# Spectra and tables of pairs requested seven slots ahead, and tables and planes in six common buffers

## The chip, the cores and the metric

The kernel runs on one core of one Trainium2 chip. The core has TensorE (PE in the profile; PEld are its weight loads), VectorE (DVE), ScalarE (ACT), GpSimd (POOL) and SyncE (SP), an SBUF of 128 partitions, PSUM banks of 2 KB a partition, and 16 DMA engines. SP and POOL issue nearly all transfers of this kernel, each on a queue of its own, in the order of their programs. The metric is the device time of one execution in microseconds; less is better.

## The reference

Two layers. The first is a long convolution by FFT with a filter that a small network makes, the second a feed-forward network (FFN) with the maximum of three products:

```python
h_filt = (np.maximum(pos_emb @ w1, 0.0) @ w2) * np.exp(-0.01 * pos)[:, None]
u = x * v                                            # (4, 12544, 128)
Uf = np.fft.rfft(u, n=2 * S, axis=1)
Hf = np.fft.rfft(h_filt, n=2 * S, axis=0)
y = np.fft.irfft(Uf * Hf[None], n=2 * S, axis=1)[:, :S]
a = (x * y).reshape(4 * 12544, 128)
h = np.maximum(np.maximum(a @ W1, a @ W2), a @ W3)   # W: 128 x 768
out = h @ w_out                                      # 768 x 128
```

Everything is float32.

## The kernel before

**The transform.** The FFT is written as matmuls. A batch's tokens are cut into 98 blocks of 128; 32 *units* of four channels each are multiplied, turned and taken through a first transform over the blocks (90 frequencies, kept as the SBUF tile `spec`). Then 45 *pairs* of frequencies (`NK = 45`) go one by one through a second transform, the product with the filter's spectrum, and the inverse of the second transform; its result is stored in DRAM (`zd`). A tile of the FFN later loads what it needs of it (`zt`), does the last inverse step and runs the FFN on 392 columns.

**The stages.** The first batch's transform stands alone, up to about 296 us. Then the main loop runs over the 32 tiles of each of batches 0, 1 and 2, with six FFN chunks a tile: 192 *slots* a batch. Beside the FFN of one batch the transform of the next is woven in, slot by slot. The last batch's FFN follows alone, from about 1780 us.

**The order is written by hand.** `conv_steps` makes a list of steps for each slot: `at(slot, late, fn, ...)` puts a function into a slot; the main loop emits a slot's FFN work first and then the slot's steps (steps with `late` 0 before those with 1). Every engine runs its instructions in that order. In a batch's 192 slots the units come first (the early part of each stage), then the pairs: `start(x)` gives pair x its slot, the same one for an even x and the odd one after it. So the pairs go two by two, about 5.1 slots from one two to the next; the first two are at slot 59 in the stage beside batch 0, at 58 in the others, the last at 175. Where this document counts j, it counts these twos, and calls each "pair j" for short.

**What a pair step needs.** `g_quarter(g, z)` (L537) does the matmuls of the second transform for pair g (L547, reads `sq` and `wt`) and the inverse for pair z = g - 3 (L557, reads `wt` and the folded product). Three transfers feed a pair:

- `w_load(x)` (L506): the table `wt` of 256 KB from DRAM, one DMA on POOL's queue for each pair; both halves are used at slot `start(x)`.
- `q_load(g, n)` (L512): the spectra `sq` of two pairs, copied within SBUF from `spec` with the parts laid on the partitions that the matmuls want; eight DMAs of 64 KB on SP's queue. It has two buffers. For g = 0 the last unit's `u_fours`, two to three slots before, must have written `spec`.
- `h_load(g, n)` (L526): the filter's spectrum `ht` of two pairs, four DMAs of 256 KB on SP's queue, two buffers, asked for one slot ahead. It is first read by VectorE's `q_re` (L591).

On SP's queue the tiles' `zt` loads stand between these (L782, L789), emitted at the first slot of a tile two tiles ahead, and their two buffers come free when `t_last` of two tiles earlier is done. On POOL's queue stand the tables, the stores `zd` (L580) and `out_dram` (L857), and the loads `xT` (L772), among POOL's own additions (L599, which wait for VectorE's L596).

**The buffers.** `wt` has a pool of three buffers. `u_planes` (L407) makes for each unit a tile of 16-bit planes from the products, which a transposing DMA (L420) reads; these have three buffers under the tag `pl`. Both kinds of tile take 2 KB a partition.

Of the kernel before, what the change touches and what calls it, by code (L numbers as in the profile page):

```python
# [10 lines left out]
FP32 = mybir.dt.float32  # L11
I32 = mybir.dt.int32
U16 = mybir.dt.uint16
# [3 lines left out]
P = 128  # L17
# [78 lines left out]
def kernel(  # L96
# [21 lines left out]
    NK = N1 // 2  # L118
# [287 lines left out]

    def u_planes(u):  # L407
        a, _ = us.pop(u)
        pl_ = cvp.tile([P, 2, 4, P], U16, tag="pl", name="planes", bufs=3)
        w = pl_[:].rearrange("p h s (e m) -> p h s e m", e=2)  # L410
        nc.gpsimd.memset(pl_[:].rearrange("p h s (e m) -> p (h s e) m", e=2)[:, :, HB:], 0)
        for h in range(2):
            nc.gpsimd.tensor_copy(  # L413
                w[:, h, :, :, 0:HB],
                a[:].bitcast(U16).rearrange("p s (m e h) -> p h s e m", e=2, h=2)[:, h])
        us[u] = pl_
# [87 lines left out]
            fn()  # L504

    def w_load(x):  # L506
        w = wp.tile([P, 2, 2, 2, 64], FP32, tag="w", name="wt")
        nc.gpsimd.dma_start(w[:].rearrange("p a k r m -> p (a k r m)"),
                            wq_d[x].rearrange("p a f -> p (a f)"))
        ws[x, 0], ws[x - LATE, 1] = w[:, 0], w[:, 1]  # L510
# [153 lines left out]
    def conv_steps(b, done):  # L664


        out = []

        def at(slot, late, fn, *args):
            out.append((slot, late, len(out), fn, args))  # L670

        for u in range(5, done):
            at(2 * (u - 4), 1, u_first, u)
        lead, low, UNIT = (-14, -NT * NF, 0.8) if b > 1 else (6, 0, 0.7)
        share = UNIT * (NU - done - 1)
        per_pair = (END - lead - 11) / (share + (NK + LATE) // 2 * 2 - 2)
        units = []
        for u in range(done, NU):  # L680
            s = (u - done) * UNIT * per_pair + lead
            load_ = max(low, int(s) - 9)
            at(load_, 0, u_load, b, u)
            mul = max(load_ + 2, int(s) - 6)
            at(mul, 0, u_mul, u, nc.gpsimd)
            at(max(mul, int(s) - 5), 0, u_planes, u)
            at(max(mul + 1, int(s) - 4), 0, u_dma, u)
            at(int(s), 0, u_join, u)
            if u % 2:
                on = int(s + 2)  # L690
                at(on, 1, u_two, u - 1)
                at(on + 1, 1, u_fours, u - 1)
                at(on + 2, 1, u_fours, u)
                units.append(on)
        s0 = on + 7

        def start(x):
            return s0 + int(x // 2 * 2 * per_pair)

        load = [0.6] * (NT * NF)  # L700
        for x in range(NK + LATE):
            s = start(x)
            load[s] -= 1.2
            load[s + 1 + x % 2] += 1.4

        def emptiest(among, cost):
            s = min(among, key=lambda i: load[i])
            load[s] += cost
            return s

        plan = []
        busy = {start(x): 2 for x in range(NK + LATE)}
        for x in range(NK + LATE):
            busy.setdefault(start(x) + 1, 1)
        for s in units:
            for k, n in enumerate((1, 3, 9, 2)):
                busy[s - 1 + k] = max(n, busy.get(s - 1 + k, 0))
        for i in range(NT - 1):
            s = i * NF
            last = min((3, 4, 2), key=lambda k: busy.get(s + k, 0))  # L720
            load[s + last] += 0.6
            if s <= s0:
                plan.append((0, 0, last))
                continue
            a = emptiest(range(s, s + 2), 0.7) - s
            plan.append((a, emptiest(range(s + a, s + max(a + 1, last - 1)), 0.7) - s, last))
        plan.append((3, 3, 4))

        for at_, fn, *args in ((11, h_load, 0, 2), (10, h_load, 2, 2),
                               (9, w_load, 0), (9, w_load, 1), (8, w_load, 2)):  # L730
            at(s0 - at_, 0, fn, *args)
        for x in range(NK + LATE):
            s, odd = start(x), x % 2
            g, z = x if x < NK else None, x - LATE if x >= LATE else None
            at(s, 1, g_quarter, g, z)
            at(s + 1 + odd, 0, g_fold, g, z)
            if x > 2:
                at(s - 4, 0, w_load, x)
            if z is not None:
                at(s + 3 + odd, 0, g_store, b, z)  # L740
            if g is None:
                continue
            if g % 2 == 0:
                at(s - 4, 0, q_load, g, min(2, NK - g))
                if g > 2:
                    at(s - 1, 0, h_load, g, min(2, NK - g))
            first = s + 2 + 2 * odd
            at(first, 0, q_swap, g, 0)
            at(first + 1, 0, q_swap, g, 64)
            last = start(x + LATE) - 1  # L750
            a = emptiest(range(first + 1, min(first + 3, last - 1) + 1), 0.7)
            at(a, 0, q_re, g)
            a = emptiest(range(a, min(first + 4, last - 1) + 1), 0.7)
            at(a, 0, q_im, g)
            two = sorted(emptiest(range(a + 1, last + 1), 0.55) for _ in range(2))
            for q in range(2):
                at(two[q], 0, q_unfold, g, q)
        slots = {}
        for s, _, _, fn, args in sorted(out, key=lambda r: r[:3]):
            slots.setdefault(s, []).append((fn, args))  # L760
        return slots, plan, s0
# [288 lines left out]
    for u in range(4, NU, 2):  # L1050
        t = uts.pop(u)
        for v in range(2):
            if u + 4 < NU:
                u_mul(u + 4 + v)
            at = 4 * (u + v)
# [23 lines left out]
    cvp = pro.enter_context(tc.tile_pool(name="cvp0", bufs=3))  # L1079
# [94 lines left out]
    for s in range(NK + 3):  # L1174
# [34 lines left out]
        if s == NK:  # L1209
            unit(0)  # L1210
            pl = sps.tile([P, 512], FP32, tag="pl", name="pl")
# [23 lines left out]
    wp = conv.enter_context(tc.tile_pool(name="wp", bufs=3))  # L1235
    hh = conv.enter_context(tc.tile_pool(name="hh", bufs=2))
    cvp = conv.enter_context(tc.tile_pool(name="cvp", bufs=3))
# [12 lines left out]
    for b in range(1, B):  # L1250
        slots, *rest = conv_steps(b, EARLY if b == 1 else 0)
        plans.append(rest)
        for s, steps in slots.items():
            besides.setdefault((b - 1) * NT * NF + s, []).extend(steps)
# [145 lines left out]
```

## Time and profile before

| | |
|---|---|
| timed runs | 2223.01, 2230.61, 2232.32 us; median 2230.61 |
| profiled execution | 2221.21 us, its span 2219.4 us, mean granted clock 0.997 |
| 0 to 296 us (first batch's transform alone) | PE busy 281.3 us, DMA share 0.84 |
| 296 to 1780 us (FFN of batches 0 to 2, transform beside it) | PE busy 1478.9 of 1484.0 us, DMA share 0.95, 211 GB/s |
| 1780 us to the end (last batch's FFN) | PE busy 433.9 of 439.4 us, DMA share 0.23 |
| groups L547 and L557 (the matmuls of pairs) | 90.6 and 86.6 us of PE, 2160 matmuls each |
| transfers, issue to landing, median | ht 7.1, wt 5.3, sq 5.6, zt 3.8 us |
| SP's queue | 274.5 MB, 56.6% of the 16 DMA engines' span |
| POOL's queue | 130.3 MB, 21.5% |

A share of busy time is the time in which an engine had an instruction running, over the span. Matmuls are pipelined and the profile models their ends, so PE's gaps are best read from starts. DMA issues are not counted as busy time of the issuing engine; the DMA share is the mean over the 16 DMA engines of the time that packets took, and can pass 1 where packets overlap.

### The profile page before, as it was taken

Reading aid. Unit: us, or ns where it says so; the run is one execution under the profiler, and the core shown is the slowest. Engines: PE = TensorE matmul, PEld = TensorE weight load, DVE = VectorE, ACT = ScalarE, POOL = GpSimd, SP = SyncE. Lnnn points to the kernel's source line nnn. Section 1 sums busy time; section 2 is a strip of 40 time slices with the busy share of each in tenths; the row PEclk is TensorE's granted clock in tenths of the full one; section 3 lists DMA queues with packets and bytes.
Section 4 is the critical chain, followed back from the end, with each engine's and each line's share of the span. In section 5 each row is a group of like instructions: output and inputs, shape, how many; then the busy total and the mean of one; then the engine's idle time right before and its main releaser. Section 6 shows DMA issues by size and latency. Waiting matters only on the chain.

```text
span 2219.4 us, 77166 instructions
## 1 busy us (share of the span) xinstructions
PE 2194.1 (99%) x31655; PEld 1297.3 (58%) x31655; DVE 1534.6 (69%) x3293; ACT 1210.9 (55%) x2223; POOL 1179.0 (53%) x1577
## 2 busy tenths in 40 slices
PE   9999999999999999999999999999999999999999
PEld 7988755555555455555555555555555545667776
DVE  5688857677877766667888766677878744554443
ACT  3699845466666555456666555556666622222222
POOL 1166567534455566544444566634454426666665
PEclk9999999999999999999999999999999999999999
DMA  8789999879999898879999999969999722222221
GB/s 196 186 264 311 291 181 196 171 191 233 247 246 241 218 188 175 168 175 245 230 256 231 229 195 178 173 158 252 236 240 238 200 79 58 59 71 69 63 58 24
DMA packets 491332, 411.62 MB, mean 185 GB/s; under 512 B 289406, under 2 KB 407920, under 8 KB 490979
## 3 DMA queue, kind: packets, MB, share of 16 engines
q1 hardware_dynamic: 443689, 274.50, 56.6%
q0 software_dynamic: 45808, 130.25, 21.5%
q8 instruction: 249, 4.08, 0.8%
q10 hardware_dynamic: 1482, 1.93, 0.4%
q14 instruction: 104, 0.85, 0.1%
HBM read 262.85 MB, written 84.67 MB: 157 GB/s over the span
## 4 chain that ended last, share of the span: by engine, by line
PE 84%; DMA 6%; DVE 3%; POOL 3%; issue 2%; SPq 1%; ACT 1%; POOLq 0%; DVEq 0%; ACTq 0%
PE hps L167 42%; PE ops L167 17%; PE ops L903 6%; PE cps L167 3%; PE cps L449 3%; PE ps L176 3%; PE cps L547 3%; PE cps L557 2%; DMA sq<-spec 2%; DMA ht<-hd 2%; DMA zt<-zd 1%; PE ps L167 1%; DMA wt<-wq_const 1%; POOL xt L638 1%; PE last L167 1%
## 5 line engine op out<-in xcount | busy, mean ns | idle before, releaser
L167 PE MATMUL hps<-gt,w_sb 128*64 128x392 f32 (+1 forms) x7672 | 1157.4, 495 | 0.8 <-DVE gt L829 0.7
L839 ACT ACTIVATE hid<-hps 128x392 f32<-128x392 f32 x768 | 382.5, 498 | 762.7 <-PE hps L167 744.9
L167 PEld LDWEIGHTS hps<-gt,w_sb 128*64 128x64 f32 (+1 forms) x7672 | 430.6, 126 | 439.1 <-issue 407.9
L842 DVE TENSOR_TENSOR hid<-hid,hps 128x392 f32<-128x392 f32 x768 | 427.8, 557 | 351.5 <-PE hps L167 335.8
L167 PE MATMUL ops<-hid,wo_sb 128*64 128x392 f32 x2304 | 476.9, 492 | 0.0
L599 POOL TENSOR_TENSOR cb<-cb,xs 128x512 f32<-128x512 f32 x135 | 177.4, 1314 | 404.9 <-DVE xs L596 389.5
L167 PEld LDWEIGHTS ops<-hid,wo_sb 128*64 128x64 f32 x2304 | 165.7, 137 | 213.5 <-issue 213.5
L572 DVE TENSOR_TENSOR cb<-cps,eo 128x512 f32<-128x512 f32 (+1 forms) x288 | 175.1, 649 | 72.8 <-ACT eo L569 71.7
L857 POOL DMA_DIRECT2D out_dram<-ot x96 | 76.3, 795 | 235.3 <-ACT ot L855 217.2
L587 ACT ACTIVATE xs<-cb 32x512 f32<-32x512 f32 x270 | 169.4, 628 | 21.5 <-DVE cb L572 12.6
L588 ACT COPY xs<-cb 32x512 f32<-32x512 f32 x270 | 166.3, 616 | 3.2
L603 DVE TENSOR_TENSOR xs<-cb 128x256 f32<-128x256 f32 x270 | 148.7, 598 | 6.5 <-POOL cb L599 6.5
L429 ACT COPY uT<-turned 113x512 uint16<-113x512 uint16 x180 | 126.0, 771 | 0.1
L386 POOL TENSOR_TENSOR ut<-ut 128x392 f32<-128x392 f32 x90 | 93.3, 1037 | 41.2 <-DMA ut<-in_vr_dram 39.2
L167 PEld LDWEIGHTS cps<-f4p,even 90*64 90x64 f32 x1552 | 87.2, 138 | 35.9 <-issue 33.2
L772 POOL DMA_DIRECT2D xT<-in_x_dram x172 | 101.1, 601 | 6.8 <-PE pt L1099 3.3
L580 POOL DMA_DIRECT2D zd<-cb x135 | 95.0, 704 | 14.6 <-DVE cb L572 10.7
L471 DVE TENSOR_TENSOR low<-high,cps 128x180 f32<-128x180 f32 x186 | 54.6, 334 | 67.6 <-ACT high L461 67.6
L928 POOL DMA_DIRECT2D out_dram<-o x120 | 72.5, 610 | 47.2 <-DVE o L921 45.7
L167 PE MATMUL cps<-f4p,zt 90*64 90x49 f32 x1552 | 95.8, 222 | 0.0
L547 PE MATMUL cps<-sq,wt 64*64 64x128 f32 x2160 | 90.6, 276 | 4.6 <-DMA wt<-wq_const 2.9
L413 POOL COPY planes<-ut 128x392 uint16<-128x392 uint16 x180 | 95.1, 564 | 0.0
(172 smaller groups left out, 3348.2 us busy)
## 6 DMA issues: line engine op xcount, KB each, us to landing
ht<-hd SPq DMA_DIRECT2D x264, 256.0 KB, 7.1
wt<-wq_const POOLq DMA_DIRECT2D x144, 256.0 KB, 5.3
zd<-cb POOLq DMA_DIRECT2D x135, 256.0 KB, 6.3
zt<-zd SPq DMA_DIRECT2D x384, 90.0 KB, 3.8
sq<-spec SPq DMA_DIRECT2D x528, 64.0 KB, 5.6
ut<-in_xr_dram SPq DMA_DIRECT2D x128, 196.0 KB, 4.3
ut<-in_vr_dram SPq DMA_DIRECT2D x128, 196.0 KB, 4.5
wt<-wt_const SPq DMA_DIRECT2D x90, 256.0 KB, 5.1
```

What stands on the lines that cost most here:

```text
L167: nc.tensor.matmul(out[h:h + w], lhsT[:, h:h + w], rhs, start=start, stop=stop, skip_group_check=True)
L429: nc.scalar.copy(uts[u][0:HR, 8 * (u % 2):8 * (u % 2) + 8].rearrange("n s r t -> n (s r t)").bitcast(U16).rearrange("n (s r t h) -> n h s ...
L547: nc.tensor.matmul(ps[64 * a:64 * a + 64, at:at + D], w[64 * r:64 * r + 64, k, a, :], t[64 * r:64 * r + 64, k, :, a], start=(k == 0), stop ...
L572: nc.vector.tensor_tensor(out=cb[:, a, lo:hi], in0=ps[:, lo:hi], in1=eo[:, lo:hi], op=op)
L587: nc.scalar.mul(xs[at:at + 32], xt[at + 32:at + 64], -1.0)
L588: nc.scalar.copy(xs[at + 32:at + 64], xt[at:at + 32])
L599: nc.gpsimd.tensor_tensor(out=xts[g], in0=xts[g], in1=xs[:], op=ALU.add)
L603: nc.vector.tensor_tensor(out=ab[:, q], in0=y[:, 0], in1=y[:, 1], op=(ALU.subtract, ALU.add)[q])
L772: eng.dma_start(xT[c * NG:(c + 1) * NG].rearrange("d i p n -> d (i p) n"), x[:, 4 * i:4 * i + 8, c, b, :])
L839: nc.scalar.activation(h[:], pa[:, 0:N], Relu)
L842: nc.vector.tensor_tensor(out=h[:], in0=h[:], in1=pb[:, 0:N], op=ALU.max)
L903: nc.tensor.matmul(ps[32 * q:32 * q + 32, 0:H2], w[:, m:m + 32], rhs[:, H2 * c:H2 * c + H2], start=start, stop=True, skip_group_check=True)
```

## The change

Three edits. The tables `wt` leave their own pool of three buffers and share six buffers (tag `pl`) with the planes, which had three; the SBUF taken is the same. `w_load` of pairs from the fourth on is put seven slots before its pair's slot, in place of four. `q_load` likewise, but for the first one of a batch, which stays at four.

```diff
     def u_planes(u):
         a, _ = us.pop(u)
-        pl_ = cvp.tile([P, 2, 4, P], U16, tag="pl", name="planes", bufs=3)
+        pl_ = cvp.tile([P, 2, 4, P], U16, tag="pl", name="planes", bufs=6)
...
     def w_load(x):
-        w = wp.tile([P, 2, 2, 2, 64], FP32, tag="w", name="wt")
+        w = cvp.tile([P, 2, 2, 2, 64], FP32, tag="pl", name="wt", bufs=6)
...
             if x > 2:
-                at(s - 4, 0, w_load, x)
+                at(s - 7, 0, w_load, x)
...
             if g % 2 == 0:
-                at(s - 4, 0, q_load, g, min(2, NK - g))
+                at(s - (7 if g else 4), 0, q_load, g, min(2, NK - g))
                 if g > 2:
                     at(s - 1, 0, h_load, g, min(2, NK - g))
```

The order of instructions on PE, VectorE and ScalarE stays the same. On SP's queue the eight DMAs of a `q_load` move, on POOL's the DMAs of `w_load`. With pairs some five slots apart, seven slots ahead of pair j+1 is about two slots ahead of pair j, so each `q_load` now stands before the `h_load` of the pair before it, where it stood behind.

## The prediction

> **What bounds the kernel now.** I read the page's busy times first, then the groups of TensorE, then the stages.
>
> ```profile
> span 2219.4 us, 77166 instructions
> ...
> PE 2194.1 (99%) x31655; PEld 1297.3 (58%) x31655; DVE 1534.6 (69%) x3293; ACT 1210.9 (55%) x2223; POOL 1179.0 (53%) x1577
> ...
> L547 PE MATMUL cps<-sq,wt 64*64 64x128 f32 x2160 | 90.6, 276 | 4.6 <-DMA wt<-wq_const 2.9
> ```
>
> TensorE is busy in 2194.1 of 2219.4 us. No edit that leaves its matmuls alone can win more than the other 25.3 us. The table of windows (three rows of it: the stages in which pairs run beside the FFN, batches 1 to 3; columns are the window, its length, then busy us per engine, granted clock, DMA share, GB/s) says how much of this lies where the change works:
>
> ```profile
> 500.00:745.00 245.00, 242.14 (x2768) 126.54 (x2764) 195.53 (x351) 159.73 (x287) 118.08 (x151) 1.00 1.00 241
> 1005.00:1250.00 245.00, 244.00 (x2800) 127.73 (x2790) 198.85 (x353) 160.50 (x288) 118.63 (x151) 1.00 0.97 242
> 1510.00:1755.00 245.00, 244.30 (x2783) 127.73 (x2779) 198.36 (x351) 160.22 (x288) 118.45 (x151) 1.00 0.98 242
> ```
>
> Two things are to be seen: TensorE idles 2.86 + 1.00 + 0.70 = 4.6 us here by the profiler, and the DMA engines are full (1.00, 0.97, 0.98). The other 20 us of idling lie elsewhere: 14.7 before 296 us, 5.6 after 1780. The change touches neither.
>
> Ends of matmuls are modelled, so I measured the loss by starts. Around an undisturbed pair the last FFN group before it starts at 578.91, the pair at 579.67, the next FFN group at 581.58: 2.67 us in all. A disturbed one, in the timeline of TensorE:
>
> ```profile
> 524.73 0.83 PE L167 MATMUL ops<-hid,wo_sb 128*64 128x392 f32 x4
> 526.59 0.76 PE L547 MATMUL cps<-sq,wt 64*64 64x128 f32 x14 [1.03 <-DMA wt<-wq_const]
> ...
> 529.07 1.54 PE L167 MATMUL hps<-gt,w_sb 128*64 128x392 f32 x8
> ```
>
> 529.07 - 524.73 = 4.34, that is 1.67 lost. The same subtraction for every pair of the three stages gives 9.0 us lost, at a dozen of some 70 pairs, all on late wt or sq. The weight loads' waits on these two tiles (7.1 and 2.8 us, 17 times) agree from above, the 4.6 us from below. So the prize is 9 us, 0.4% of the span.
>
> **The change, part by part.** *The w load.* Its POOL stream around the pair above:
>
> ```profile
> 515.49 1.27 POOL L599 TENSOR_TENSOR cb<-cb,xs 128x512 f32<-128x512 f32 x1 [1.16 <-DVE xs L596]
> 516.90 0.79 POOL L857 DMA_DIRECT2D out_dram<-ot  x1
> 517.68 1.13 POOL L508 DMA_DIRECT2D wt<-wq_const  x2
> ```
>
> Three slots earlier, the two loads move ahead of the second L599 and its 1.16 us wait, usually of a zd or out store too, and come right behind the first (510.09, 1.27 us long): about 511.4 in place of 517.7, 6.3 us sooner. They land a median 5.6 us after issue (9.8 at most). Issue at 517.68 and the last landing at 528.0 missed 525.5, when TensorE was ready, by 2.5 us; now it is early by 3.8. No other pair's wt was later, so all wt waits go. The two issues (1.13 us) then delay the second L599 by nothing: it waits for VectorE longer than that, 1.16.
>
> *The sq load.* The SP queue, same stretch:
>
> ```profile
> 503.42 1.97 SPq L531 DMA_DIRECT2D ht<-hd  x4
> 506.14 1.79 SPq L782 DMA_DIRECT2D zt<-zd  x2
> 507.97 9.11 SPq L520 DMA_DIRECT2D sq<-spec  x8
> 517.18 2.06 SPq L531 DMA_DIRECT2D ht<-hd  x4
> 521.64 1.77 SPq L782 DMA_DIRECT2D zt<-zd  x2
> 523.46 9.52 SPq L520 DMA_DIRECT2D sq<-spec  x8
> ```
>
> Eight issues of 0.6 us last 7 to 9.5 us: each SP DMA waits for the one of eight semaphores that it raises itself, so for the eighth DMA before it to land. The queue is a line that is served at the pace of the DMA engines; who is put ahead gains what the overtaken loses. In the changed program's SP stream the eight sq DMAs of pair j+1 stand before the four ht DMAs of pair j (in some pairs before a zt too) instead of behind. In the trace's semaphore events of the three stages an ht DMA lands 1.3 us behind the one before it, an sq DMA 0.7 (means). So sq gains 4 x 1.3 = 5.2 us, and ht loses 8 x 0.7 = 5.7. The sq landings now lie from 0.9 us late to 9.7 early; with 5.2 added none is late. Its two buffers don't forbid this: the one asked for is free once pair j-1 is done, 13 us before pair j, while SP comes to it about 8 us before.
>
> *What is late next: ht.* First reader is L591, 9.2 to 12.2 us after its pair's first matmul; ht lands 1.2 to 5.8 us after that matmul, 4.5 to 9.1 us early. Less 5.7, this is from 1.2 late to 3.4 early, about one pair in six late. Behind L591 on VectorE stand L596 and the FFN's maximum L842, which frees a PSUM bank that TensorE wants two slots on:
>
> ```profile
> 522.55 0.68 DVE L591 TENSOR_TENSOR cb<-cb,ht 128x512 f32<-128x512 f32 x1
> 523.15 0.68 DVE L596 TENSOR_TENSOR xs<-xs,ht 128x512 f32<-128x512 f32 x1
> 523.76 0.55 DVE L842 TENSOR_TENSOR hid<-hid,hps 128x392 f32<-128x392 f32 x1
> ```
>
> L842 ends at 524.31; the slot that needs its bank starts at 525.39 (524.73 + 0.66, the pitch of a group of four). The cover is 1.1 us, so a lateness of 1.2 costs 0.1 and eleven of them 1.1. I take 0.5 us in all, since the two sides of each swap are only means. Ends: 0, and 53 us, if ht in all eleven pairs landed as slowly as the slowest of its transfers (12.3 us against a median of 7.6): (4.7 + 1.2 - 1.1) x 11. The near end is the likelier, as ht follows on sq in both orders and meets the same queue.
>
> *zt* is asked for as soon as its buffer is free and read 11 to 15 us after it lands: nothing, whoever passes it.
>
> *Six common buffers.* At most four wt live at once (two of a pair, two of the next), and planes of the next batch begin at slot 173 on buffers whose pair was at 165, so nobody waits. POOL's three waits of 6.8 us for a wt buffer at the stages' heads go; nothing on the path stood behind them. Cost 0.
>
> *g = 0* stays at four slots; the first sq of a stage lands 0.4 to 2.5 us early as before.
>
> Sum in the profiled execution: 2221.2 (its own time) - 9.0 + 1.0 (waits that stay, ends 0 and 4.4, the half that I show only by starts) + 0.5 = 2213.7.
>
> One rule weighs on the cover: the Trainium skill, "DMA: Bandwidth & Descriptors", section Specifications, gives a core some 358 GB/s of HBM. By it the 241 GB/s above leave a third spare, no load would be late for ever, and the sum would be 2212. The same page, section Queues, rings and completion order, lets each DMA engine take turns between the queues' rings, so what is asked sooner takes turns from the rest. The rows side with the second: a share of 0.97 to 1.00 at 241 GB/s.
>
> **To the median.** The three timed runs are 2223.0, 2230.6 and 2232.3, the profiled one is 2221.2: the median lies 9.4 above it. The clock was 1.00 throughout these stages and TensorE's work is fixed; the lateness of transfers is what the trace shows to vary. If the 9.4 us are more of the same waits they go too (2213.7); if not, they stay (2223.1). Nothing tells which; I take the middle: **2218.4 us**, 0.5% less than 2230.6. I call 0.5% what can be told from no change here.
>
> **The rivals.**
> - *The waits go, but the 9.4 stay* (0.35): 2223, 0.3% less, within the bound. For it: the prize seen is 9 us. Against: a spread of 9 us needs a source in an otherwise fixed stream.
> - *The DMA engines are the limit* (0.09): the same bytes at the same 241 GB/s, so TensorE waits as long, only for others: 2228 to 2231. For it: the share of 1.00. Against, from SP's waits in 500 to 745 (total us, times, longest): the queue did stand before zt until TensorE freed the buffer, 16 of 245 us, so the line has some 6% to give.
>
> ```profile
> SPq L782 <- PE hps L167: 16.0, 15, 3.9
> ```
>
> - *ht takes over and the end is slower* (0.11): place L591, price its lateness less 1.1 us. Reckoned is 0.8 early in the mean (6.5 less 5.7). If it lands 3 us later than that in half of the 66 pairs, each loses 3 - 0.8 - 1.1 = 1.1, together 36 us against 8.5 won: 2258. The gain is gone at 2.2 us later (0.26 per pair), and 2242, 0.5% slower, is reached at 2.5. For it: 4.5 early less 5.7 is negative, and 1.1 us is all that covers. Against: the wait at zt lets the line drain, and the SP line as a whole is no longer than before.
>
> **Numbers.** Forecast 0.45, the rivals 0.35, 0.09 and 0.11. The forecast's own range is 2212 to 2221; 0.40 of its chance is under 2219.5, faster by over 0.5%, as is 0.08 of the first rival's: 0.48. Within: 0.05 + 0.27 + 0.09 = 0.41. Slower: 0.11. The range for 8 in 10 begins at the floor, 2212.2 (2221.2 - 9.0), less 2 for the distance of the profiled run to the fastest timed one, and ends at the last timed run: 2210 to 2232.
>
> **What would show it.** The group of L547 should idle under 1 us on DMA, the SP queue should show sq ahead of ht, landings of sq should be 5 us or more early. A wait of L591 on ht, or of hps matmuls on L842, would show the third rival; a DMA share still at 1.00 with new waits on wt the second. The middle of the 9.4 us is the weakest step.

## The result, and the profile after

The changed kernel is slower by half a per cent: 2239.88 us (median of 8 runs, 2234.49 to 2247.95) against 2230.91 us for the kernel before, run beside it (8 runs, 2223.01 to 2235.88). The ratio is 1.005, with a 95% interval of 1.0033 to 1.0066. The forecast of 2218.4 us and its whole range, 2210 to 2232, lie below it. The profiled execution took 2240.94 us, its span 2239.1 us. It lies near the median of its kernel, while the profiled execution before (2221.21) was faster than all 8 runs beside it, so the two profiles are 19.7 us apart where the medians are 9.0 apart.

From the start of the first pair (447.2 us before, 449.2 after) to that of the last (1766.9 and 1786.7) the three stages beside the FFN took 1319.7 us before and 1337.5 after: 17.8 of the 19.7 us between the two profiled executions. So the loss lies where the change works. The same table of windows as in the prediction, for the kernel after (columns: window, length, busy us of PE, PEld, DVE, ACT and POOL with their instructions, granted clock, DMA share, GB/s), with two short windows that I come back to:

```profile
500.00:745.00 245.00, 243.85 (x2802) 127.08 (x2798) 196.71 (x351) 160.97 (x290) 118.37 (x151) 1.00 0.99 238
1005.00:1250.00 245.00, 240.31 (x2762) 125.37 (x2760) 194.05 (x345) 155.00 (x278) 116.97 (x150) 0.99 0.97 232
1510.00:1755.00 245.00, 237.71 (x2700) 123.77 (x2698) 191.49 (x339) 154.20 (x277) 115.72 (x148) 0.99 0.99 234
1662.00:1665.00 3.00, 3.00 (x32) 1.52 (x24) 1.64 (x3) 0.30 (x1) 1.65 (x2) 0.51 0.81 227
1666.00:1669.00 3.00, 3.00 (x22) 1.30 (x20) 2.21 (x4) 1.74 (x3) 2.05 (x4) 1.00 1.05 273
```

TensorE idles 1.15 + 4.69 + 7.29 = 13.1 us in the three long windows, where it idled 4.6, and the DMA engines are as full as before while they move less (238, 232 and 234 GB/s against 241 and 242): the pairs come more slowly, not the bytes faster. What TensorE waited for, in the view of waits (us in total, times, longest):

```profile
PE cps L557 <- DVE xs L603: 15.3, 18, 2.6
PE cps L547 <- DMA sq<-spec: 1.6, 2, 0.9
```

No wait on wt is left, and little on sq; before, L547 waited 2.9 us on wt and 1.4 on sq. In their place stands a wait that was 0.5 us before: L557, the inverse transform, waits for L603, VectorE's last step of the product with the filter. The page's groups name what stands behind it (after the last bar: idle time before the group, and what ended most of it):

```profile
L591 DVE TENSOR_TENSOR cb<-cb,ht 128x512 f32<-128x512 f32 x135 | 92.4, 684 | 30.5 <-DMA ht<-hd 13.4
...
L557 PE MATMUL cps<-xs,wt 64*64 64x128 f32 x2160 | 88.0, 275 | 15.4 <-DVE xs L603 15.3
```

L591 is the first reader of ht, the filter's spectrum. One such place, first in the timeline of VectorE, then POOL's, then TensorE's (start, length, engine, what it does, and in brackets the idle time before it and what ended it):

```profile
1657.94 0.69 DVE L591 TENSOR_TENSOR cb<-cb,ht 128x512 f32<-128x512 f32 x1 [3.21 <-DMA ht<-hd]
1658.55 0.69 DVE L596 TENSOR_TENSOR xs<-xs,ht 128x512 f32<-128x512 f32 x1
1659.15 0.56 DVE L842 TENSOR_TENSOR hid<-hid,hps 128x392 f32<-128x392 f32 x1
1659.63 0.56 DVE L829 TENSOR_TENSOR gt<-cps,xT 128x392 f32<-128x392 f32 x1
1660.10 1.86 DVE L603 TENSOR_TENSOR xs<-cb 128x256 f32<-128x256 f32 x4
```

```profile
1644.26 1.15 POOL L508 DMA_DIRECT2D wt<-wq_const  x2
...
1646.95 1.28 POOL L599 TENSOR_TENSOR cb<-cb,xs 128x512 f32<-128x512 f32 x1 [0.83 <-DVE xs L596]
...
1659.41 1.26 POOL L599 TENSOR_TENSOR cb<-cb,xs 128x512 f32<-128x512 f32 x1 [4.82 <-DVE xs L596]
```

```profile
1657.74 0.67 PE L547 MATMUL cps<-sq,wt 64*64 64x128 f32 x16
1661.01 0.78 PE L557 MATMUL cps<-xs,wt 64*64 64x128 f32 x16 [2.61 <-DVE xs L603]
...
1662.05 1.10 PE L557 MATMUL cps<-xs,wt 64*64 64x128 f32 x16
1663.08 2.69 PE L167 MATMUL hps<-gt,w_sb 128*64 128x392 f32 x8
```

The ht of the pair that started at 1644.2 lands at 1657.8, 13.6 us after that start. VectorE had stood idle before L591 for 3.21 us. But the L557 at 1661.01 does not need this ht. `g_quarter` does the inverse for z = g - 3, so this L557 belongs to the pair of frequencies one before, and it waits for the L603 of that one. Counted in the order of the program, the first two of the four L603 at 1660.10 are its own. Their input, the product of the L599 at 1646.95, was ready at 1648.2. They only stood behind the late L591 in VectorE's order, with L596, L842 and L829 between. The first of them was held up once more: while POOL runs an L599, an L603 takes 1.34 us in place of 0.41 (medians of 63 and 207 in this trace), and this one ended at 1660.96, 0.3 us after the L599 beside it. L557, due at 1658.4 right after L547, starts 2.61 us late. So VectorE's 3.21 us have a cover of only 0.6 us here.

The same reading of all 18 waits gives 13 of this kind, with 13.9 of the 15.3 us: the product that L603 needed had been ready for 8 to 13 us, and L603 stood behind the L591 of a later pair. Late ht stops TensorE through the order of VectorE's instructions.

After the stall shown the clock falls: 0.51 in the window from 1662 to 1665 against 1.00 four us later, and the eight hps matmuls at 1663.08 take 2.69 us, where the same group took 1.50 at 1655.65. The records of the clock show two such dips in the three stages, of 3.41 us each at half the clock, at 1163.7 and 1662.0, and none before the change: 2 x 1.7 us more.

The waits of TensorE rose from 4.8 us (2.9 + 1.4 + 0.5) to 16.9, the dips cost 3.4: 15.5 of the 17.8 us. Why ht is late, SP's queue shows:

```profile
1640.75 4.47 SPq L520 DMA_DIRECT2D sq<-spec  x5
1647.08 2.97 SPq L531 DMA_DIRECT2D ht<-hd  x4
1650.16 1.74 SPq L789 DMA_DIRECT2D zt<-zd  x4
1654.40 7.10 SPq L520 DMA_DIRECT2D sq<-spec  x8
```

SP asks for this ht 2.9 us after its pair's start, behind the next pair's spectra; and 2.8 us earlier, at 1644.26 (the POOL line above), the next pair's two tables were asked for, so that 512 KB of tables and 1 MB of ht travel together.

### The profile page after: what moved, and what is told of

Its sections match the earlier page's. It is cut to its first block, busy times and chain, and to the rows that moved or that the text cites. A ratio compares the mean times of both kernels' runs of the same rounds, so it can differ in the third digit from the quotient of the medians.

```text
span 2239.1 us, 77219 instructions
## 1 busy us (share of the span) xinstructions
PE 2200.8 (98%) x31655; PEld 1296.9 (58%) x31655; DVE 1536.7 (69%) x3293; ACT 1211.0 (54%) x2223; POOL 1179.5 (53%) x1577
## 4 chain that ended last, share of the span: by engine, by line
PE 76%; DMA 11%; DVE 5%; issue 3%; POOL 3%; SPq 2%; ACT 1%; DVEq 0%; POOLq 0%; ACTq 0%
PE hps L167 38%; PE ops L167 15%; PE ops L903 6%; DMA ht<-hd 5%; PE cps L167 3%; PE cps L449 3%; PE ps L176 3%; DMA sq<-spec 2%; DMA zt<-zd 2%; PE cps L557 2%; PE cps L547 2%; PE ps L167 2%; POOL xt L638 1%; DVE xs L603 1%; SPq L520 1%
## 5 line engine op out<-in xcount | busy, mean ns | idle before, releaser
L842 DVE TENSOR_TENSOR hid<-hid,hps 128x392 f32<-128x392 f32 x768 | 428.5, 558 | 342.9 <-PE hps L167 324.6
L599 POOL TENSOR_TENSOR cb<-cb,xs 128x512 f32<-128x512 f32 x135 | 176.3, 1306 | 383.5 <-DVE xs L596 349.3
L857 POOL DMA_DIRECT2D out_dram<-ot x96 | 77.4, 806 | 271.4 <-ACT ot L855 245.6
L603 DVE TENSOR_TENSOR xs<-cb 128x256 f32<-128x256 f32 x270 | 149.1, 600 | 7.3 <-POOL cb L599 7.3
L591 DVE TENSOR_TENSOR cb<-cb,ht 128x512 f32<-128x512 f32 x135 | 92.4, 684 | 30.5 <-DMA ht<-hd 13.4
L557 PE MATMUL cps<-xs,wt 64*64 64x128 f32 x2160 | 88.0, 275 | 15.4 <-DVE xs L603 15.3
```

The lines of the kernel that those rows point to most:

```text
L557: nc.tensor.matmul(ps[64 * k:64 * k + 64, at:at + D], w[64 * a:64 * a + 64, k, q, :], ab[64 * a:64 * a + 64, q, k, :], start=(g is None an ...
L599: nc.gpsimd.tensor_tensor(out=xts[g], in0=xts[g], in1=xs[:], op=ALU.add)
L603: nc.vector.tensor_tensor(out=ab[:, q], in0=y[:, 0], in1=y[:, 1], op=(ALU.subtract, ALU.add)[q])
L842: nc.vector.tensor_tensor(out=h[:], in0=h[:], in1=pb[:, 0:N], op=ALU.max)
```

## Experiments

Three theories stood at the start. **A, order:** ht is late because it now stands behind the next pair's spectra in SP's queue; the tables do nothing. **B, buffers:** planes and tables wait for one another in the six common buffers. **C, the DMA engines are the limit:** who is early makes another late, and no order gains. After the first set of runs A was replaced by **E:** ht is late only where both hold, the place behind the spectra and tables that travel beside it. The kernels of a set ran on one chip with runs of the kernel before beside them. The median before was 2229.23 us (28 runs) in the first set, 2222.34 (29) in the second, 2225.04 (17) in the third, so ratios are compared, not medians of different sets.

### First set: the parts, and a filter asked for sooner

**e1_tables:** tables at seven slots, six common buffers, spectra at four.

```diff
-                at(s - (7 if g else 4), 0, q_load, g, min(2, NK - g))
+                at(s - 4, 0, q_load, g, min(2, NK - g))
```

> Only the tables go seven slots ahead, in the six common buffers; the spectra stay at four. Theory A (the spectra put before the filter's spectrum make ht late, and L557 waits for L603 behind it): SP's order is that of before, so L591 waits for ht under 1 us in all and L557 for L603 about 1 us as before; the waits for wt (two thirds of the 9 us of before) go: 2224 to 2229 where before is 2231, ratio 0.997 to 0.999. Rival B (the common buffers, or tables asked for sooner, take DMA time from the rest): part of the loss is here already, ratio 1.002 or more. Rival C (the DMA engines are the limit whatever the order): waits for sq take the place of those for wt, ratio 0.999 to 1.001.

**e2_spectra:** the kernel before with the spectra's edit alone.

```diff
-                at(s - 4, 0, q_load, g, min(2, NK - g))
+                at(s - (7 if g else 4), 0, q_load, g, min(2, NK - g))
```

> Only the spectra go seven slots ahead; the tables stay at four slots in their own three buffers. Theory A: the whole loss of the change is here, and the wt waits of before stay: L557 waits 12 us or more for L603, ratio 1.004 to 1.009. Rival B: at or under before, ratio 0.997 to 1.000. Rival C: ratio 0.999 to 1.001.

**e3_filter_first:** the change, with ht asked for three slots ahead, so that it stands before the next pair's spectra again.

```diff
-                    at(s - 1, 0, h_load, g, min(2, NK - g))
+                    at(s - 3, 0, h_load, g, min(2, NK - g))
```

> The whole change, and the filter's spectrum is asked for three slots ahead in place of one, so that it stands before the spectra of the next pair again. Theory A: ht is late no more (L591 waits for it under 2 us in all), L557 waits under 3 us for L603, and the spectra land 5 us early as in the change: ratio 0.995 to 0.999. Rival B: the loss stays, 1.003 or more. Rival C: new waits for sq or ht of 5 to 10 us, ratio 0.999 to 1.002.

**e4_five:** the change with spectra at five slots, which also puts ht first.

```diff
-                at(s - (7 if g else 4), 0, q_load, g, min(2, NK - g))
+                at(s - (5 if g else 4), 0, q_load, g, min(2, NK - g))
```

> Tables seven ahead in the common buffers, spectra five ahead: sooner by one slot, but still behind the filter's spectrum of the pair before. Theory A: what hurts is the overtaking, not the asking sooner, so L591 does not wait and the time is that of the tables alone or better, ratio 0.995 to 0.999. Rival B as for the tables alone. Rival D (each slot sooner costs a third of the loss): ratio 1.001 to 1.003.

| | median us | ratio, 95% interval |
|---|---|---|
| e1_tables | 2224.20 | 0.9982, 0.9965 to 0.9999 |
| e2_spectra | 2221.98 | 0.9967, 0.9954 to 0.9980 |
| e3_filter_first | 2218.27 | 0.9954, 0.9941 to 0.9968 |
| e4_five | 2235.43 | 1.0024, 1.0012 to 1.0037 |

Each part alone is a gain (the tables by a hair: the interval ends at 0.9999); together they are a loss. A falls with e2: there ht stands behind the spectra as in the change, and the kernel is faster. e4 is a miss of A too (0.995 to 0.999 was expected), and rival D's range, 1.001 to 1.003, held it; but what is late in e4 is another transfer than in the change, as its waits show, and e2 and e3 with spectra at seven speak against a price by the slot. C falls with e3: the same bytes in another order, and TensorE has no gap left in the three windows, at 244, 244 and 241 GB/s. The windows of e3, and its waits:

```profile
500.00:745.00 245.00, 245.00 (x2822) 128.14 (x2822) 200.62 (x358) 162.94 (x292) 121.13 (x153) 1.00 0.98 244
1005.00:1250.00 245.00, 245.00 (x2838) 128.67 (x2834) 200.24 (x357) 161.79 (x291) 120.58 (x154) 1.00 1.02 244
1510.00:1755.00 245.00, 245.00 (x2824) 128.40 (x2818) 201.22 (x356) 160.84 (x289) 120.38 (x153) 1.00 0.99 241
```

```profile
PE cps L547 <- DMA sq<-spec: 2.3, 2, 1.2
PE cps L557 <- DVE xs L603: 0.5, 2, 0.2
```

PE is busy 245.00 of 245 us in each; the two waits that stay, 2.3 us, are the first pairs of stages, whose spectra (g = 0) no edit here touches. The waits of TensorE in e1, in e2 (second fence) and in e4 (third):

```profile
PE cps L547 <- DMA sq<-spec: 10.2, 11, 2.1
```

```profile
PE cps L547 <- DMA wt<-wq_const: 4.2, 3, 2.7
PE cps L557 <- DVE xs L603: 2.8, 4, 1.2
```

```profile
PE cps L547 <- DMA sq<-spec: 9.2, 10, 1.9
```

With the tables alone sooner the spectra are what is late, with the spectra alone the tables are. In e2 the wait behind a late ht is there (2.8 us), but small. e1's profile is the slowest of its 12 runs (2233.3 us; the median is 2224.2), so its 10.2 us overstate what its median pays; e4's is near its own median (2234.86). In e4 the view puts 3.6 us more of L547's waits down to zt and zd, which L547 does not read; the spectra land up to 2.3 us late there and the tables 3 us early or more, so these too are waits on spectra, 12.8 us in all. Why one slot on the spectra puts e4's median 11 us above e1's, these profiles don't tell: it stays open.

### Second set: what the tables do to ht

**e5_nine:** the change with tables at nine slots, so that they are asked for ahead of ht and not beside it.

```diff
-                at(s - 7, 0, w_load, x)
+                at(s - 9, 0, w_load, x)
```

> The whole change, but the tables are asked for nine slots ahead in place of seven, so that they travel beside the spectra (issued 20 us or more before their pair) and not beside ht. Theory E (two delays add up on ht: it stands behind the spectra, and the tables asked for at seven slots take turns from it; in the change 132 of 207 ht DMAs have a table beside them, with the spectra alone moved 71 of 216): ht's mean margin comes back from 3.0 to about 4.4 us, and the time to that of the spectra alone, ratio 0.995 to 0.999. Rival F (asking for tables sooner takes DMA time whenever it is): 1.004 or more.

**e6_buffers:** spectra at seven, six common buffers, tables at four as before.

```diff
-                at(s - 7, 0, w_load, x)
+                at(s - 4, 0, w_load, x)
```

> Spectra seven ahead, six common buffers, but the tables at four slots as before. Theory E: the buffers are innocent, so this is the run of the spectra alone again, ratio 0.995 to 0.998. Rival B (the common buffers): 1.002 or more.

**e7_no_store:** the change, less traffic on POOL's queue. It leaves out the stores of the results of batches 0 to 2 except the last tile of each.

```diff
-        nc.gpsimd.dma_start(dst, o[:])
+        if i[1] == NT - 1:
+            nc.gpsimd.dma_start(dst, o[:])
```

> The whole change, without the stores of the FFN's result in batches 0 to 2 except for each batch's last tile (196 KB a tile less on POOL's queue, some 6% of the bytes of the full stage). Theory E, as far as it rests on shared DMA engines: ht's mean margin grows by 1 us or more, the pairs whose L591 finds no ht yet fall from 19 to 8 or fewer, ratio 0.995 to 0.999. If order alone decides and not the load: the margin stays at 3 and the ratio at 1.003 to 1.006.

**e8_filter_four:** e3 with tables at four slots.

```diff
-                at(s - 7, 0, w_load, x)
+                at(s - 4, 0, w_load, x)
```

> Filter's spectrum three slots ahead and spectra seven, in the order filter, spectra; tables at four slots in the six common buffers. Theory E: ht and sq have room as in the run with the filter's spectrum first, but the tables land as late as before, so L547 waits 3 to 6 us for wt: ratio 0.996 to 0.999, between that run (0.9954) and before. If the tables don't matter once ht is early: 0.9954 again.

| | median us | ratio, 95% interval |
|---|---|---|
| e5_nine | 2223.09 | 1.0000, 0.9991 to 1.0009 |
| e6_buffers | 2218.85 | 0.9978, 0.9965 to 0.9991 |
| e7_no_store | 2220.33 | 0.9987, 0.9974 to 1.0000 |
| e8_filter_four | 2233.37 | 1.0059, 1.0041 to 1.0078 |

B falls with e6: it has the change's buffers and its spectra, and is faster than before. e6 and the change differ in one number, the slot of the tables, and so do e5 and the change; both ways of moving the tables off ht remove the loss, and so does leaving out stores (e7). That the stores' bytes are what e7 gains from is likely and not shown: without them POOL also issues less and no longer waits for their data (L857). e5 missed its 0.995 to 0.999: it wins nothing besides. Its 5.2 us of waits on spectra stand at heads of stages (the longest, 2.9 us, at 447.7), where g = 0 keeps its four slots, and two of them are followed by 3.41 us at half clock (451.5 and 956.7). The waits of L557 on L603 go from 15.3 us to these (e6, then e7):

```profile
PE cps L557 <- DVE xs L603: 0.5, 2, 0.3
```

```profile
PE cps L557 <- DVE xs L603: 3.2, 6, 1.4
```

e8 is a miss as well: 0.996 to 0.999 was expected. Its waits, then POOL's and SP's queues at one of them:

```profile
PE cps L547 <- DMA wt<-wq_const: 13.1, 13, 2.6
```

```profile
1532.32 1.15 POOL L508 DMA_DIRECT2D wt<-wq_const  x2
```

```profile
1530.92 1.89 SPq L531 DMA_DIRECT2D ht<-hd  x4
1533.22 9.37 SPq L520 DMA_DIRECT2D sq<-spec  x8
```

The tables and the ht of one pair are now asked for within 1.4 us of each other, and then the next pair's spectra follow; here it is the tables that have no time to lose. TensorE was ready 7 us after they were asked for and got them 2.45 us later, in its own timeline:

```profile
1541.81 1.12 PE L547 MATMUL cps<-sq,wt 64*64 64x128 f32 x14 [2.45 <-DMA wt<-wq_const]
```

It is the collision of E from the other side: two loads meet, and the one with less margin is late.

The place of each transfer in time, from the trace's semaphore events: means over the 57 twos of pairs with j of 4 and more, in us after the start of the pair that ht belongs to (L591 wants it about 10.4 after). The next pair starts some 13.5 after, so a table that leads its own pair by 13.6 is asked for at -0.1. The last column counts the pairs in which ht landed within 0.3 us of L591's start.

| | first ht asked for | last ht landed | next tables asked for | L591 waited |
|---|---|---|---|---|
| before | -6.2 | 3.9 | 4.9 | 0 |
| after | -2.2 | 8.2 | -0.1 | 19 |
| e9_change (the change again) | -3.3 | 6.4 | -0.2 | 13 |
| e1_tables | -6.1 | 3.7 | -0.3 | 0 |
| e2_spectra | -4.0 | 6.1 | 4.9 | 6 |
| e3_filter_first | -9.7 | 0.0 | -0.1 | 0 |
| e4_five | -4.6 | 5.4 | -0.4 | 6 |
| e5_nine | -4.9 | 4.9 | -8.4 | 4 |
| e6_buffers | -4.9 | 4.9 | 5.0 | 0 |
| e7_no_store | -3.7 | 5.8 | -0.1 | 7 |
| e8_filter_four | -8.5 | 1.8 | 4.6 | 0 |

The two runs of the change differ by 1.8 us in where ht lands, and e2 and e6, which ask in the same order at the same slots, by 1.2, so smaller differences in this column mean nothing. What tells the change apart is the last column: 19 and 13 against 0 to 7. In the change the next tables are asked for some 2 to 3 us after ht, while it travels; in e6 the tables come when ht has landed, in e5 they come ahead of it. With the same order on SP, ht then lands at 4.9 in place of 8.2 or 6.4, and L591 finds it missing in 0 or 4 pairs in place of 19 or 13. In e1 and e3 ht is ahead of the tables by 5.8 and 9.6 us, and they don't hurt it. In e3 they travel where nothing is near its time: from 0, when ht has landed, to about 5, when the next ht has only just been asked for (-9.7 + 13.5 = 3.8). Of the 3.3 us between e6 and the change (its first run), 2.7 are there when ht is asked for: SP begins on the spectra ahead of it 1.4 us later, and their eight issues take 7.4 us in place of 6.1. Which of the tables' bytes delays which of SP's transfers the events don't say.

### Third set: the change again, the best again, and ht asked for later

**e9_change** is the change, **e10_filter_first** is e3, both once more, beside each other.

> The change itself once more, beside the other three on one chip. All theories: slower than before as at first, 1.003 to 1.007, with L557 the group that waits.

> The change with the filter's spectrum asked for three slots ahead, once more: ratio 0.994 to 0.998 again, and 0.7 to 1.2% under the change in the same call. If the first run of it owed its gain to the chip it ran on: 0.999 to 1.003.

**e11_swap:** the kernel before, with ht asked for three slots later, behind the next pair's spectra, and nothing sooner.

```diff
-                    at(s - 1, 0, h_load, g, min(2, NK - g))
+                    at(s + 2, 0, h_load, g, min(2, NK - g))
```

> Before, with nothing asked for sooner and the filter's spectrum three slots later (two slots behind its pair's start), so that it stands behind the next spectra as in the change. Theory E: the place in the line alone makes ht late: its mean margin falls from 6.5 to 1 us or less, L557 waits 10 us or more for L603, ratio 1.004 to 1.020. If the place in the line is innocent: margin 4 us or more, ratio 0.998 to 1.002.

**e12_first_nine:** e3 with tables at nine slots.

```diff
-                at(s - 7, 0, w_load, x)
+                at(s - 9, 0, w_load, x)
```

> Filter's spectrum three slots ahead, spectra seven, tables nine. Theory E: all three feeds land early through the full stage and no pair waits; what is left is the first pair of each stage, where nine slots put tables beside the first spectra: 1 to 3 us late there, once a stage. Ratio 0.994 to 0.998, within 0.2% of the run with the tables at seven. If asking sooner costs in itself: 0.3% or more above that run.

| | median us | ratio, 95% interval |
|---|---|---|
| e9_change | 2236.18 | 1.0057, 1.0040 to 1.0074 |
| e10_filter_first | 2216.26 | 0.9963, 0.9949 to 0.9978 |
| e11_swap | 2274.69 | 1.0235, 1.0212 to 1.0258 |
| e12_first_nine | 2222.76 | 0.9990, 0.9980 to 1.0001 |

The change repeats its loss, with the same wait (12.8 us on L603), and the version with ht first repeats its gain: it beats both kernels, 0.4% under the one before and 0.9% under the change (2216.26 / 2236.18 = 0.991). Its SP queue asks for the ht of the pair that starts at 1655.1, then for zt, then for the next pair's spectra:

```profile
1645.12 1.75 SPq L531 DMA_DIRECT2D ht<-hd  x4
1646.98 2.34 SPq L789 DMA_DIRECT2D zt<-zd  x4
1649.58 9.82 SPq L520 DMA_DIRECT2D sq<-spec  x8
```

e11 shows a late ht and its price more plainly than the change does:

```profile
DVE cb L591 <- DMA ht<-hd: 41.2, 18, 6.5
PE cps L557 <- DVE xs L603: 20.9, 16, 3.1
PE cps L547 <- DMA wt<-wq_const: 12.7, 11, 2.2
```

ht lands 10.0 us after its pair's start, 6.1 later than before, and L591 finds it missing in 26 pairs of 57, with tables at four slots. So E's "only where both hold" is too narrow: the place in the line can do it without the tables. The kernel is 2.35% slower, far worse than e2, where ht also stands behind the spectra. The reason stands in SP's own waits on TensorE for a free zt buffer (e11, then e2):

```profile
SPq L789 <- PE cps L167: 103.6, 32, 7.2
```

```profile
SPq L789 <- PE cps L167: 34.6, 16, 5.1
```

A slot only gives a request its place in SP's program; SP runs that program ahead until something stops it, and a zt whose buffer is still in use stops it. Three slots later, ht comes to stand behind such a zt as well, as here in e11 for the pair that starts at 1569.6:

```profile
1560.93 7.39 SPq L520 DMA_DIRECT2D sq<-spec  x8
1568.43 4.59 SPq L789 DMA_DIRECT2D zt<-zd  x4
1573.06 2.96 SPq L531 DMA_DIRECT2D ht<-hd  x4
```

So e11 does not price the swap with the spectra by itself. What asking sooner wins is in part a place ahead of the zt that waits.

e12 is a miss, by little (0.994 to 0.998 was expected): at nine slots the tables are asked for 22.0 us before their pair, 8.5 before the start of the pair ahead, beside that pair's ht (at -7.2), and the spectra that follow on SP come late: 5.6 us of waits on them at L547, 3.9 of these at the heads of the three stages as expected, where e10 has 3.0 in all. That the tables make them late is likely, and was not tried by itself; and 2.6 us are not the 6.5 between the two medians, whose rest stays open.

## Why the prediction was wrong

**"wt 6.3 us sooner, all waits go", "sq gains 5.2, none is late":** right. The change leaves 1.6 us of waits on sq and none on wt; past the heads of the stages the spectra land 3.4 us early at least, the tables 2.6.

**The prize of 9.0 us:** too large in the profiled execution. e3 and e10, with nearly all waits gone, need 1314.4 and 1316.6 us from first to last pair against 1319.7: 5.3 and 3.1 us.

**"The two issues then delay the second L599 by nothing":** here the first step failed. The tables were priced as two instructions of POOL, and what their 512 KB do to the transfers beside them got no term. The prediction costed the two edits one by one and added them; the runs show 0.9982 for the one, 0.9967 for the other, and 1.005 for both.

**"ht loses 8 x 0.7 = 5.7 ... about one pair in six late":** the step that failed most. As a mean 5.7 was too much: with the spectra alone moved ht lands 2.2 us later than before (e2: 6.1 against 3.9), in the change 4.3 (e9: 2.5). But means were not what counted. The prediction shifted every landing by one amount, which left no pair more than 1.2 us late. In the change 19 of 57 pairs find no ht, VectorE idles up to 3.2 us before their L591, 28.5 us in all, and ht lands as much as 15.0 us after its pair's start where L591 wants it at 10.4. The line lags for several pairs on end: at 1077 to 1177 us eight in a row land at 10.1 to 13.9. Even with the cover of 1.1 us taken off each, these 19 would have cost 11.5 us.

**"The cover is 1.1 us":** the smaller fault, in the path more than in the size. I followed VectorE's queue from L591 to L842 and on to a PSUM bank. The next line of that same timeline is the one that TensorE waits for first:

```profile
524.23 2.35 DVE L603 TENSOR_TENSOR xs<-cb 128x256 f32<-128x256 f32 x4
```

The first of these four belongs to the pair of frequencies before, and ended at 525.57. Without the wait on wt its L557 would have been due at some 526.0 (TensorE ready at 525.5, and L557 0.49 behind L547 as at 579.67): a cover of 0.4. In the five places after the change that lost most, idle time before L591 less idle time before L557 gives 0.5 to 1.1. That `g_quarter` does the inverse for z = g - 3 in a later pair's slot was plain in the code.

**"I take 0.5 us in all":** the mis-sized term. It measured 14.8 us more waiting at L557 (15.3 against 0.5) and 3.4 us at half the clock, which had no term. Put into the sum with the 2.7 us that the waits at L547 really gave (4.3 to 1.6): 2221.2 - 2.7 + 14.8 + 3.4 = 2236.7, against 2240.9 measured; the other 4.2 us stay unaccounted for. Its far end, 53 us, held it, and so did the third rival (0.11), which named L591 and the lateness of ht, but it asked for half of 66 pairs (19 of 57 came), with the cover of 1.1 us and the wrong path behind it.

**"Six common buffers: cost 0":** right (e6).

**The 9.4 us between profile and median:** probably more waits of the kind, as half assumed. With them gone, e3's 6 runs span 2.2 us (2217.5 to 2219.7), where 28 of the kernel before, beside them, span 18 (2223.6 to 2241.7). Only one execution of each was profiled, so it is not shown.

## What to carry to other kernels

In this kernel, with the DMA engines full, a request moved forward made late what travels beside it, whether in its own queue or in another: price a prefetch by its bytes and by the margin of whatever it meets, and price two such edits together. Price the lateness by the worst stretch and not by the mean. Before a cover is put at some size, look also at what stands behind the late reader on its own engine: here the work that TensorE missed first did not read the late tile at all. And a slot in a hand-written order is a place in a queue, not a time: what a request stands behind decides when it starts. The gain here lay in asking for each load in the order in which it is read, with none beside another that has no margin: ht first, then the spectra, with the tables at seven slots.

## What the hardware showed unexpectedly

A stall of TensorE of under 3 us can cost 1.7 us more. After the gaps (from start to start) of 2.88 and 2.58 us at 1658.1 and 1160.3 the clock stood at half for 3.41 us; in e1 after one of 2.42 us, in e5 after one of 1.83; but in e2 one of 3.22 us passed without, in e11 one of 3.36, and in e4 one of 2.13. In e11 there were eight dips between the first pair and the last, of 3.41 or 6.83 us, one of them (1047.0) after no gap longer than 1.4 us, and its mean clock was 0.989. The Trainium skill, "TensorE: Matmul & The Clock Gate", Part 1, describes a clock that is halved and released by windows of some 3.4 us that run freely. The length of the dips agrees with it (3.41 and twice that), and free windows would explain why longer gaps passed, which no run here shows; that a gap shorter than a window is enough at times, the runs add.
